# One whole load of the spatial bias, later MLP weights and regrouped token tiles in a planned two-layer kernel

## The chip, the cores and the metric

The kernel runs on one core of a Trainium2 chip. The metric is the device time of one execution in microseconds (us). The core has five engines with an instruction stream each: TensorE (PE, matrix products; its weight loads are listed apart as PEld), VectorE (DVE), ScalarE (ACT, activation functions), GpSimd (POOL) and SyncE (SP), which here issues all DMA transfers. Each engine works through its own stream strictly in the order in which it was written; streams meet through semaphores.

## The reference

Two layers follow each other, each an attention block and a gated MLP, both behind a layer norm and both added to x. The attention has 32 query heads of 16 columns that share one key and one value head. The MLP mixes tokens: one half of its GELU output is normalised and multiplied by a token-by-token matrix w_sp, to which a bias b_sp, one number for each token, is added. The same weights serve both layers.

```python
B, S, D, H = (1, 2048, 512, 32)          # Dh = 16, F = 1792, Fh = 896, all bf16
def _A_ref(x, wq, wk, wv, wo):
    q = (x @ wq).reshape(B, S, H, Dh)    # to b h s d
    k = x @ wk
    v = x @ wv
    scores = einsum('bhqd,bkd->bhqk', q, k) * Dh ** (-0.5)
    o = einsum('bhqk,bkd->bhqd', softmax(scores), v)
    return o.reshape(B, S, H * Dh) @ wo
def _B_ref(x, w_in, w_sp, b_sp, w_out):
    z = gelu(x @ w_in)
    z1 = z[..., :Fh]
    z2 = layernorm(z[..., Fh:])
    g = einsum('ts,bsf->btf', w_sp, z2) + b_sp[None, :, None]
    return (z1 * g) @ w_out
x = A_x
for _ in range(2):
    x = x + _A_ref(layernorm(x), A_wq, A_wk, A_wv, A_wo)
    x = x + _B_ref(layernorm(x), B_w_in, B_w_sp, B_b_sp, B_w_out)
```

## The kernel before

**An order written by a planner.** The Python code does not write instructions one after the other. It makes tasks with costs, dependencies and priorities, and a planner (`Sched`, `Kernel.run`) steps through a clock of its own, gives each free engine its next task, and so fixes the order of every engine's stream. On the chip only this order and the semaphores count. A table `PLAN` changes the planner's settings for single stretches of 1.25 us of its clock; it has some thousand rows. Some tasks have a gate: they may be placed only after a point of the planner's clock, such as `W_FROM` (the weights wo, w_in, w_out) and `WSP_FROM` (w_sp and the bias).

**Attention.** 2048 tokens are 16 tiles of 128. They are cut into chunks (`CHUNKS`), each chunk into units of 512 columns (tokens times head groups), 32 units a layer. A unit has 64 score blocks of 128 x 512, four for each tile of keys. PE computes up to four blocks side by side (L2468) into PSUM banks. About two thirds of the blocks go to ACT, which takes the exponential of two banks (L2666) or of one (L2665). The others go to DVE, which makes three integer ramps that together approximate the exponential: the first from PSUM (L2557, an "A" block), the other two by DVE or POOL from the first (L2577, L2561; two or four at once). All results land in a ring of P slots, `NPS` of 1 KB a partition (`Pb`). PE multiplies them by V, four at once in a "round" (L2725, PV). A finished unit is copied out of PSUM (oT, L1959), transposed by DMA (oP, L1634), divided by its denominators (L2105 on DVE, L2122 on POOL), transposed again (onT), multiplied by wo (L2065) and added to x. Then the second layer norm follows and a transpose into xnT. At the head of each layer the first layer norm's result xn is transposed by DMA into the space of z1 (`z<-xn`, L1634; the first two tiles on PE), and keys, values and queries are made from it (L1871, L1874, L1901).

**MLP stages.** When the chunks of a group (`GROUPS`) are through, an MLP stage runs for the group's tokens: PE multiplies by w_in (L2161 for z2, L2222 for z1) and ACT takes GELUs (L2166, L2236). Its table of functions is changed before and after (L2968). z1 is made for up to 512 tokens at a time, but never across a multiple of 512 tokens, since z1 and g lie in four token blocks tc. During a stage PE does not take up new scores. z2 is normalised (DVE L2174, POOL L2189) and kept in a ring of eight tiles (`Z2R`).

**Passes over w_sp.** The sum over the tokens s is cut into passes of two to four tiles (`PASSES`). A pass can start when its last group is through its stage. For each of the four token blocks tc and each of seven feature blocks f, PE multiplies the pass's z2 tiles by a slab of w_sp that DMA has brought in transposed (wstr, L1642), and DVE adds the result to g (L2290, `gp`). These products fill the gaps that attention leaves on PE. In the first pass the add takes the bias instead of the old g: `bspc` holds 512 tokens of it for all partitions, in one buffer, so that its four loads a layer (`L1627`) wait for one another:

```python
if pi == 0:
    lb = self.dma(self.bspc[:], self.B_b_sp[tc * 512:(tc + 1) * 512].partition_broadcast(P), 131072,
                  self.bs_use, prio=2, tag="ldb", gate=lambda: self.s.t > self.WSP_FROM)
```

The last pass of a layer (L2319, L2321, L2329, L2340) multiplies by z1, then w_out follows (L2350) and the add to x (L2354).

**SP's queue around the change.** In the program before, SP issues 13 of the 14 first transposes `z<-xn`, then wo, w_in, the last `z<-xn`, w_out, two oP, one onT, a slab of w_sp, the first quarter of the bias and another slab of w_sp. PE, DVE and SP keep this order whatever comes late.

Of the kernel before, what the change touches and what calls it, by code (L numbers as in the profile page):

```python
# [30 lines left out]
CHUNKS = (((0,128),(128,128),(256,256),(512,512),(1024,256),(1280,128),(1408,128),(1536,256),(1792,128),(1920,128)), ((0,128),(128,128),(256,256),(512,512),(1024,256),(1280,128),(1408,128),(1536,256),(1792,128),(1920,128)))  # L31
# [3 lines left out]
GROUPS = (((0,1,2),(3,),(4,5),(6,7),(8,9)), ((0,1,2),(3,),(4,5),(6,7),(8,9)))  # L35
PASSES = (((0,4),(4,8),(8,11),(11,14),(14,16)), ((0,4),(4,8),(8,11),(11,14),(14,16)))
# [34 lines left out]
def c_mm(n, cols):  # L71
# [15 lines left out]
    20: dict(SLACK_HI=800, FILL_MIN=4, PV_MAX=4, DVE_LEAD=300, POOL_TOP=2500, QUADP=0),
    21: dict(SLACK=350, PV_EFF=0.8),
    22: dict(SLACK=350, PV_LEAST=4, PV_EFF=0.8),
    23: dict(SLACK=350, ACT_LOW=700, PV_LEAST=4, PV_EFF=0.8, COLS=0),  # L90
    24: dict(SLACK=350, ACT_LOW=1400, PV_LEAST=4, PV_EFF=0.8, COLS=0),
    25: dict(SLACK=200, DVE_LEAD=-300, POOL_TOP=2500, SCORE_CAP=5),
    26: dict(SLACK=200, DVE_LEAD=-300, POOL_TOP=3500, SCORE_CAP=5),
    27: dict(SLACK=200, DVE_LEAD=-300, POOL_TOP=3500, SCORE_CAP=5),
    28: dict(SLACK=200, DVE_LEAD=-300, POOL_TOP=3500, MISC_T=700, ACT_MAX=1, SCORE_CAP=5),
    29: dict(SLACK=200, DVE_LEAD=-300, MISC_T=700, ACT_MAX=1, SCORE_CAP=5),
    30: dict(SHARE=0.31, POOL_TOP=2500),
    31: dict(SHARE=0.45, POOL_TOP=2500, QUADP=0),
    32: dict(FILL_MIN=4, PV_EFF=0.8),
    33: dict(PV_LEAST=4, QUADP=0),  # L100
    34: dict(PV_LEAST=4, QUADP=0),
    35: dict(PV_LEAST=4, SHARE=0.4, MISC_T=2500, QUADP=0),
    36: dict(ACT_LOW=1700, PV_LEAST=4, PV_EFF=0.8, SHARE=0.4, MISC_T=2500, DVE_HIGH=2400, QUADP=0),
    37: dict(ACT_LOW=1700, PV_LEAST=4, PV_EFF=0.8, SHARE=0.4, POOL_TOP=2500, MISC_T=2500, DVE_HIGH=2400, QUADP=0),
    38: dict(ACT_LOW=1700, PV_LEAST=4, PV_EFF=0.8, SHARE=0.4, POOL_TOP=2500, MISC_T=2500, SCORE_CAP=5, DVE_HIGH=2400, QUADP=0),
    39: dict(ACT_LOW=1700, PV_LEAST=4, PV_EFF=0.8, SHARE=0.45, POOL_TOP=2500, MISC_T=2500, SCORE_CAP=5, DVE_HIGH=2400, QUADP=0, QUADD=0),
    40: dict(PV_LEAST=8, SHARE=0.31, SCORE_CAP=7, DVE_HIGH=1200),
    42: dict(PV_LEAST=4),
    43: dict(SLACK_HI=300, PV_EFF=0.8, MISC_T=700, DVE_HIGH=1200),
    44: dict(SLACK_HI=300, PV_EFF=0.8, MISC_T=700, DVE_HIGH=1200),  # L110
    45: dict(SLACK_HI=300, PV_EFF=0.8, MISC_T=700, DVE_HIGH=1200),
    46: dict(SLACK_HI=300, PV_EFF=0.8, POOL_TOP=2500, MISC_T=2500, DVE_HIGH=2400),
    47: dict(POOL_TOP=2500),
    48: dict(POOL_TOP=2500),
    49: dict(FILL_BUSY=3, DVE_LEAD=-300, HOLD=400),
    51: dict(FILL_BUSY=3, SHARE=0.28, POOL_TOP=3500, HOLD=400),
    52: dict(FILL_BUSY=3, SHARE=0.28, POOL_TOP=3500, HOLD=400, ACT_MAX=1),
    53: dict(POOL_TOP=7000),
    54: dict(POOL_TOP=7000),
    55: dict(SLACK=450, SLACK_HI=400, PV_LEAST=8, POOL_TOP=3500, SCORE_CAP=7),  # L120
    56: dict(SLACK=450, SLACK_HI=400, PV_LEAST=8, POOL_TOP=3500, SCORE_CAP=7),
    57: dict(SLACK=450, SLACK_HI=400, PV_LEAST=8, POOL_TOP=3500, SCORE_CAP=7),
    58: dict(SLACK=450, SLACK_HI=400, ACT_LOW=1400, PV_LEAST=8, POOL_TOP=3500, SCORE_CAP=7, QUADD=0),
    59: dict(SLACK=450, SLACK_HI=650, ACT_LOW=1400, PV_MAX=1, PV_LEAST=8, POOL_TOP=3500, SCORE_CAP=7, QUADD=0),
    60: dict(SLACK=450, SLACK_HI=650, ACT_LOW=1400, FILL_BUSY=3, PV_MAX=1, PV_LEAST=8, POOL_TOP=3500, SCORE_CAP=7, DVE_HIGH=1200, QUADD=0),
    61: dict(SLACK=450, SLACK_HI=650, ACT_LOW=1400, FILL_BUSY=3, PV_MAX=1, PV_LEAST=8, POOL_TOP=3500, SCORE_CAP=7, DVE_HIGH=1200, QUADD=0),
    63: dict(ACT_MAX=1),
    64: dict(ACT_LOW=900, PV_MAX=4, SHARE=0.28, HOLD=0, MISC_T=700),
    65: dict(MISC_T=2500, COLS=0),
    66: dict(COLS=0),  # L130
    67: dict(COLS=0),
    68: dict(PV_MAX=3),
    69: dict(ACT_LOW=700, PV_MAX=3, DVE_HIGH=1200),
    70: dict(ACT_LOW=700, PV_MAX=3, MISC_T=2500, ACT_MAX=1, DVE_HIGH=1200),
    72: dict(SLACK=200, ACT_LOW=500, PV_MAX=1, DVE_LEAD=300, POOL_TOP=7000),
    73: dict(SLACK=200, ACT_LOW=1700, PV_MAX=4, DVE_LEAD=300, POOL_TOP=3500),
    74: dict(ACT_LOW=1700, PV_MAX=3, DVE_LEAD=300, POOL_TOP=3500),
    75: dict(ACT_LOW=1050, PV_MAX=1, POOL_TOP=2500, HOLD=400, QUADD=0),
    76: dict(ACT_LOW=1400, PV_MAX=1, POOL_TOP=2500, HOLD=400, QUADD=0),
# [24 lines left out]
    106: dict(ACT_LOW=1050, SHARE=0.4, POOL_TOP=2500, HOLD=400, DVE_HIGH=2400),
    107: dict(SLACK_HI=300, PV_MAX=4, PV_EFF=0.8),
    108: dict(SLACK_HI=300, PV_MAX=4, PV_EFF=0.8, POOL_TOP=2500),
    109: dict(SLACK_HI=300, PV_MAX=4, PV_EFF=0.8, POOL_TOP=2500, SCORE_CAP=5),
    110: dict(SLACK=600, SLACK_HI=650, FILL_MIN=3, SHARE=0.45),
    111: dict(SLACK=450, SLACK_HI=650, FILL_MIN=3, SHARE=0.45, QUADP=0),
    112: dict(SLACK=350, SLACK_HI=650, FILL_MIN=3, SHARE=0.45, COLS=3300, QUADP=0),  # L170
    113: dict(SLACK=350, SLACK_HI=650, FILL_MIN=3, SHARE=0.45, POOL_TOP=7000, COLS=3300, QUADP=0),
    114: dict(SLACK=350, SLACK_HI=650, FILL_MIN=3, PV_LEAST=4, SHARE=0.45, POOL_TOP=7000, COLS=3300, QUADP=0),
    115: dict(SLACK=350, SLACK_HI=650, FILL_MIN=3, PV_LEAST=4, SHARE=0.45, POOL_TOP=7000, COLS=3300, QUADP=0),
    116: dict(SLACK=350, SLACK_HI=650, ACT_LOW=1400, FILL_MIN=3, PV_LEAST=4, SHARE=0.45, POOL_TOP=7000, COLS=3300, DVE_HIGH=1200, QUADP=0),
    117: dict(SLACK_HI=800, FILL_MIN=3, POOL_TOP=3500, SCORE_CAP=7),
    118: dict(SLACK_HI=800, FILL_MIN=3, DVE_LEAD=300, POOL_TOP=3500, SCORE_CAP=7),
    119: dict(SLACK_HI=800, FILL_MIN=3, DVE_LEAD=300, POOL_TOP=3500, ACT_MAX=1, SCORE_CAP=7),
    121: dict(SLACK_HI=800, POOL_TOP=3500),
    122: dict(SLACK_HI=800, PV_EFF=0.8, POOL_TOP=3500, MISC_T=2500),
# [1283 lines left out]
class Kernel:  # L1463
# [794 lines left out]
    def spatial(self, B, pi, final):  # L2258
# [5 lines left out]
        for tc in range(4):  # L2264
# [6 lines left out]
            else:  # L2271
# [4 lines left out]
                for f in range(NF):  # L2276
# [17 lines left out]
                    if pi == 0:  # L2294
                        self.bs_use.append(outs[0])
# [873 lines left out]
```

## Time and profile before

| what | value |
|---|---|
| median of three runs (lowest, highest) | 1503.27 us (1502.33, 1505.92) |
| the profiled execution | 1499.42 us, span 1497.7 us |
| score blocks to ACT: L2666, two at a time | 1212 instructions, 1154.3 us busy |
| score blocks to ACT: L2665, one at a time | 339 instructions, 205.8 us busy |
| score blocks to DVE: L2557 | 1333 instructions, 858.2 us busy |
| z1 on PE, L2222 of 512, 384, 256, 128 columns | 112, 56, 112, 56 matmuls; 25.6, 9.9, 12.9, 3.5 us busy |
| bias loads | 8 of 128 KB, 3.7 us each from issue to landing |
| w_in and w_out loads | 1792 KB in 9.1 us, 896 KB in 7.2 us |
| first matmul of the first MLP stage | at 213.5 us |

A group of the profile names the line, the engine, the output and input tiles, the shapes and the count, then the busy time and the idle time before it. "Idle before" is time in which the engine stood still in front of that instruction, and the releaser behind the arrow is what ended the wait. Matmuls overlap, so busy time divided by count is shorter than the mean duration of one. The granted clock is the share of full speed that the clock of PE had in a window. The two long chains in the time are the attention of layer 0, to about 695 us, and of layer 1, to about 1436 us; behind each lies the rest of the MLP.

### The profile page before, as it was taken

The numbers are of one execution on the slowest core, as the hardware profiler recorded it, in microseconds if no ns is written. First come the engines' busy times: TensorE is split into PE (matmuls) and PEld (weight loads), VectorE is DVE, ScalarE is ACT, GpSimd is POOL, SyncE is SP. The second block draws the span as 40 slices with busy tenths as digits, with TensorE's granted clock in tenths as the row PEclk, the third lists the DMA queues.
The fourth block names the chain that finished last, engine by engine and source line by source line (L and its number), as shares of the span: only waits on it lengthen the run. The fifth ranks groups of instructions, "written<-read, shape, count | busy, mean of one in ns | idle before, by whom it ended". The sixth has DMA issues, their size and how long they took to land.

```text
span 1497.7 us, 35502 instructions
## 1 busy us (share of the span) xinstructions
PE 1433.2 (96%) x14120; PEld 473.1 (32%) x14120; DVE 1383.0 (92%) x2605; ACT 1377.4 (92%) x1725; POOL 1037.3 (69%) x1152
## 2 busy tenths in 40 slices
PE   8999899999999999999999988999999999999999
PEld 3332232222322322233643322322223223222345
DVE  8899998999899999989767999899998999999886
ACT  7999999999999999996589999999999999999950
POOL 6677768878688688864114767677776786888737
PEclk9999999999999999999999999999999999999999
DMA  4420001112011111112121001001111111211111
GB/s 111 114 43 12 9 18 26 26 26 40 18 26 33 23 32 30 37 20 40 21 41 32 16 12 16 15 23 26 26 37 19 30 33 19 44 30 28 28 33 57
DMA packets 156627, 47.55 MB, mean 32 GB/s; under 512 B 148913, under 2 KB 155953, under 8 KB 156465
## 3 DMA queue, kind: packets, MB, share of 16 engines
q1 hardware_dynamic: 156464, 45.28, 15.2%
q8 instruction: 115, 1.88, 0.5%
q14 instruction: 48, 0.39, 0.1%
HBM read 6.98 MB, written 2.10 MB: 6 GB/s over the span
## 4 chain that ended last, share of the span: by engine, by line
ACT 53%; PE 36%; DVE 7%; DMA 2%; issue 0%; POOL 0%; SPq 0%; DVEq 0%
ACT Pb L2666 46%; PE ps_all L2725 9%; PE ps_all L2468 9%; PE ps_all L2280 7%; ACT Pb L2665 6%; DVE Pb L2557 4%; PE ps_all L2161 3%; PE ps_all L2350 3%; PE ps_all L2222 3%; PE ps_all L2321 1%; DMA bspc<-in_B_b_sp_dram 1%; DVE Pb L2577 1%; DMA z<-xn 1%; DVE gp L2290 1%; ACT L2968 1%
## 5 line engine op out<-in xcount | busy, mean ns | idle before, releaser
L2666 ACT ACTIVATE Pb<-ps_all 128x1024 bf16<-128x1024 f32 x1212 | 1154.3, 1138 | 12.8 <-PE ps_all L2468 11.9
L2577 POOL TENSOR_SCALAR Pb<-Pb 128x1024 int16<-128x1024 int16 (+1 forms) x732 | 803.4, 1097 | 212.0 <-DVE Pb L2577 163.4
L2557 DVE TENSOR_SCALAR Pb<-ps_all 128x512 int16<-128x512 f32 x1333 | 858.2, 684 | 39.7 <-PE ps_all L2468 33.6
L2468 PE MATMUL ps_all<-z,kT 32*128 32x512 bf16 x4096 | 535.8, 385 | 45.3 <-ACT Pb L2666 25.4
L2725 PE MATMUL ps_all<-Pb,V 128*32 128x512 bf16 x6762 | 531.9, 385 | 4.2 <-DVE Pb L2557 1.0
L2468 PEld LDWEIGHTS ps_all<-z,kT 32*128 32x128 bf16 x4096 | 136.2, 91 | 570.6 <-ACT Pb L2666 393.5
L2280 PE MATMUL ps_all<-wstr,z 128*128 128x512 bf16 x784 | 224.1, 384 | 1.8 <-DVE gp L2290 1.4
L2665 ACT ACTIVATE Pb<-ps_all 128x512 bf16<-128x512 f32 x339 | 205.8, 719 | 6.1 <-PE ps_all L2468 5.9
L2577 DVE TENSOR_SCALAR Pb<-Pb 128x1024 int16<-128x1024 int16 (+1 forms) x451 | 195.7, 471 | 0.4
L2725 PEld LDWEIGHTS ps_all<-Pb,V 128*32 128x32 bf16 x6762 | 124.6, 94 | 225.9 <-issue 119.5
L2290 DVE TENSOR_TENSOR gp<-ps_all,gp 128x512 f16<-128x512 f32 x168 | 113.2, 683 | 1.2 <-PE ps_all L2280 0.8
L2280 PEld LDWEIGHTS ps_all<-wstr,z 128*128 128x128 bf16 x784 | 51.5, 97 | 93.8 <-issue 41.7
L1724 POOL TENSOR_SCALAR ln_rs<-ln_mv 128x1 f32<-128x1 f32 (+2 forms) x52 | 11.6, 225 | 97.2 <-DVE ln_mv L1734 90.4
L2561 POOL TENSOR_SCALAR Pb<-Pb 128x512 int16<-128x512 int16 x79 | 48.8, 617 | 40.3 <-DVE Pb L2577 22.3
L2350 PE MATMUL ps_all<-w_out,z 128*128 128x512 bf16 x224 | 58.4, 380 | 0.3 <-DVE z L2329 0.2
L2122 POOL TENSOR_TENSOR o_norm<-oP,rdn 128x128 bf16<-128x128 bf16 (+1 forms) x84 | 39.7, 495 | 21.4 <-DVE Pb L2577 12.1
L2161 PE MATMUL ps_all<-w_in,xnT 128*128 128x448 bf16 x256 | 53.2, 353 | 0.9 <-ACT xnT L1785 0.7
L2222 PE MATMUL ps_all<-xnT,w_in 128*128 128x512 bf16 (+3 forms) x336 | 51.5, 308 | 0.0
L2174 DVE BATCH_NORM_STATS2 st<-z 128x6 f32<-128x448 bf16 x64 | 35.6, 604 | 13.8 <-ACT z L2166 13.6
L1959 DVE CAST oT<-ps_all 128x512 bf16<-128x512 f32 x64 | 43.9, 686 | 4.2 <-PE ps_all L2725 4.1
L1733 DVE BATCH_NORM_STATS2 ln_st<-X 128x6 f32<-128x512 bf16 x64 | 43.3, 682 | 1.7 <-DMA X<-in_A_x_dram 1.5
L2236 ACT ACTIVATE z<-ps_all 128x512 bf16<-128x512 f32 (+2 forms) x62 | 31.4, 562 | 13.7 <-PE ps_all L2222 13.6
(76 smaller groups left out, 768.4 us busy)
## 6 DMA issues: line engine op xcount, KB each, us to landing
out_dram<-X SPq DMA_DIRECT2D x16, 128.0 KB, 1.7
w_in<-in_B_w_in_dram SPq DMA_DIRECT2D x1, 1792.0 KB, 9.1
X<-in_A_x_dram SPq DMA_DIRECT2D x3, 512.0 KB, 7.8
bspc<-in_B_b_sp_dram SPq DMA_DIRECT2D x8, 128.0 KB, 3.7
oP<-oT SPq DMA_TRANSPOSE x60, 2.4
w_out<-in_B_w_out_dram SPq DMA_DIRECT2D x1, 896.0 KB, 7.2
wstr<-in_B_w_sp_dram SPq DMA_TRANSPOSE x40, 4.1
X<-in_A_x_dram SPq DMA_DIRECT2D x2, 256.0 KB, 3.2
```

The costliest lines, as they stand in the source:

```text
L2161: ins = e.matmul(self.ps32[:, b, 0:448], self.xnT2[:, buf, kd, o:o + P], self.w_in[:, kd, FH + h * 448:FH + (h + 1) * 448], start=(kd == 0 ...
L2222: ins = e.matmul(self.ps32[:, b, i * nq:(i + 1) * nq], self.w_in[:, kd, f * P:(f + 1) * P], self.xnT2[:, buf, kd, x0:x0 + nq], start=(kd = ...
L2280: ins = e.matmul(self.ps32[:, b, :], self.z2[:, (s0 + i) % Z2R, f * P:(f + 1) * P], self.wstr[:, sl[i // SLAB][1] + i % SLAB, :], start=(i ...
L2290: return Task("dve", c_ps(512), lambda e: e.tensor_tensor(self.gp[:, tc, f, :], self.ps32[:, bank(), :], src, ALU.add), dps, self.GP_P, ta ...
L2350: ins = e.matmul(self.ps32[:, b, :], self.z1[:, tc, f, o:o + P], self.w_out[:, f, :], start=(f == 0), stop=(f == NF - 1))
L2468: ins = e.matmul(self.ps32[:, jb[i].i, :], self.kT[32 * j:32 * j + 32, u.half, kt * P:(kt + 1) * P], q, tile_position=(32 * j, 0), start=T ...
L2557: return lambda e: e.tensor_scalar(self.Pi[:, dst(), :], self.ps32[:, bank, :], EBIAS + lo, lo, op0=ALU.add, op1=ALU.max)
L2561: return lambda e: e.tensor_scalar(self.Pi[:, dst(), :], self.Pi[:, src(), :], lo, 1.0, op0=ALU.add, op1=ALU.mult)
L2577: return lambda e: e.tensor_scalar(self.several(self.Pi, dst), self.several(self.Pi, src), lo, 1.0, op0=ALU.add, op1=ALU.mult)
L2665: return e.activation(self.Pb[:, ss[0], :], self.ps32[:, bs[0], :], ACTF.Exp, scale=ESCALE)
L2666: return e.activation(self.two(self.Pb, *ss), self.two(self.ps32, *bs), ACTF.Exp, scale=ESCALE)
L2725: ins = e.matmul(self.ps32[32 * j:32 * j + 32, u.bank.i, :], self.V[:, var, kt, :], self.Pb[:, sl.i, :], tile_position=(0, 32 * j), start= ...
```

## The change

The bias is loaded once for the whole kernel, all 2048 tokens (512 KB), into a buffer four times as large; the first pass reads its quarter from it. The P ring shrinks from 44 to 41 slots. wo may be placed from 48,000 ns of the planner's clock instead of 45,000, and w_in and w_out, like the bias, from 75,000. The planner's cost of a w_sp transfer on SP is another formula. Chunks, groups and passes are cut anew, in both layers: the groups were 4, 4, 3, 3 and 2 tiles (the bounds in tokens 512, 1024, 1408, 1792, 2048) and are 3, 4, 4, 3 and 2 (384, 896, 1408, 1792, 2048); the passes are the same tiles. No chunk of 512 tokens is left. `PLAN` has other rows. Since the planner places everything again, the whole order differs.

```diff
-CHUNKS = (((0,128),(128,128),(256,256),(512,512),(1024,256),(1280,128),(1408,128),(1536,256),(1792,128),(1920,128)), ...
+CHUNKS = (((0,128),(128,256),(384,128),(512,256),(768,128),(896,128),(1024,256),(1280,128),(1408,128),(1536,256),(1792,128),(1920,128)), ...
-GROUPS = (((0,1,2),(3,),(4,5),(6,7),(8,9)), ((0,1,2),(3,),(4,5),(6,7),(8,9)))
-PASSES = (((0,4),(4,8),(8,11),(11,14),(14,16)), ((0,4),(4,8),(8,11),(11,14),(14,16)))
+GROUPS = (((0,1),(2,3,4),(5,6,7),(8,9),(10,11)), ((0,1),(2,3,4),(5,6,7),(8,9),(10,11)))
+PASSES = (((0,3),(3,7),(7,11),(11,14),(14,16)), ((0,3),(3,7),(7,11),(11,14),(14,16)))
 PLAN = {
...
 }
...
-    W_FROM = 45000
-    NPS = 44
+    W_FROM = 48000
+    NPS = 41
...
-        self.bspc = self.sb([P, 512], BF16, "bspc")
+        self.bspc = self.sb([P, S], BF16, "bspc")
...
     def dma_w(self, dst, src, nbytes, deps=(), prio=5, tag="dmat", gate=None):
         def cost():
-            occ = 1000 + nbytes / 610.0
+            occ = 1230 + 600 * max(0.0, nbytes / 131072 - 2.7)
...
         self.ldo = self.dma(self.wo[:], self.A_wo.rearrange("(c p) n -> p c n", p=P), 524288, prio=2.5, gate=late)
-        self.ldin = self.dma(self.w_in[:], self.B_w_in.rearrange("(kd p) f -> p kd f", p=P), 1835008, prio=2.5, gate=late)
-        self.ldout = self.dma(self.w_out[:], self.B_w_out.rearrange("(c p) n -> p c n", p=P), 917504, prio=2.5, gate=late)
+        def later():
+            return s.t > self.WSP_FROM
+        self.ldin = self.dma(self.w_in[:], self.B_w_in.rearrange("(kd p) f -> p kd f", p=P), 1835008, prio=2.5, tag="ldb", gate=later)
+        self.ldout = self.dma(self.w_out[:], self.B_w_out.rearrange("(c p) n -> p c n", p=P), 917504, prio=2.6, tag="ldb", gate=later)
+        self.ldbs = self.dma(self.bspc[:], self.B_b_sp.partition_broadcast(P), 524288, prio=2.4, tag="ldb", gate=later)
...
                 if pi == 0:
-                    lb = self.dma(self.bspc[:], self.B_b_sp[tc * 512:(tc + 1) * 512].partition_broadcast(P), 131072,
-                                  self.bs_use, prio=2, tag="ldb", gate=lambda: self.s.t > self.WSP_FROM)
-                    self.bs_use = []
+                    lb = self.ldbs
...
-                        src = self.bspc[:] if pi == 0 else self.gp[:, tc, f, :]
+                        src = self.bspc[:, tc * 512:(tc + 1) * 512] if pi == 0 else self.gp[:, tc, f, :]
...
-                    if pi == 0:
-                        self.bs_use.append(outs[0])
```

More of the change, by code (lines that the diff above doesn't have):

```diff
@@ L87 @@
[L87 to L103, printed above, removed]
@@ L1127 @@
-    1190: dict(SLACK=150, ACT_LOW=900, PV_LEAST=4),
+    1: dict(FILL_MIN=4),
+    2: dict(FILL_MIN=4),
+    3: dict(FILL_MIN=4),
+    4: dict(FILL_MIN=4),
+    5: dict(FILL_MIN=4),
+    6: dict(FILL_MIN=4),
+    7: dict(FILL_MIN=4),
+    8: dict(FILL_MIN=4),
+    9: dict(ACT_LOW=900),
+    10: dict(ACT_LOW=900),
+    11: dict(ACT_LOW=900, COLS=3300, QUADP=0),
+    12: dict(ACT_LOW=700, FILL_BUSY=3, COLS=3300, QUADP=0),
+    13: dict(ACT_LOW=1700, PV_EFF=0.8),
+    15: dict(SLACK=600),
+    16: dict(SLACK=600, POOL_TOP=2500, HOLD=400, SCORE_CAP=5),
@@ new lines @@
+    158: dict(ACT_MAX=1),
+    159: dict(FILL_BUSY=3),
+    160: dict(SLACK_HI=800, PV_LEAST=4),
+    161: dict(SLACK_HI=800, ACT_LOW=1050, PV_LEAST=4, ACT_MAX=1, SCORE_CAP=5),
+    162: dict(ACT_LOW=700, PV_MAX=4, POOL_TOP=2500, HOLD=0),
+    164: dict(SHARE=0.24, MISC_T=700),
+    165: dict(SHARE=0.24, MISC_T=700),
+    166: dict(FILL_BUSY=4, HOLD=400),
+    167: dict(MISC_T=700),
+    168: dict(MISC_T=700),
+    169: dict(PV_MAX=1, PV_EFF=0.8),
+    171: dict(ACT_LOW=500),
+    172: dict(ACT_LOW=900, DVE_LEAD=300),
@@ new lines @@
+    191: dict(SCORE_CAP=5),
+    192: dict(SCORE_CAP=5),
+    193: dict(PV_MAX=1, MISC_T=2500, SCORE_CAP=5),
+    194: dict(SLACK=350, FILL_MIN=4, SCORE_CAP=5, COLS=3300),
+    195: dict(SLACK=350, FILL_MIN=4, PV_LEAST=4, DVE_LEAD=-300, COLS=3300, DVE_HIGH=2400),
+    196: dict(POOL_TOP=3500),
+    197: dict(ACT_LOW=900, PV_LEAST=8, POOL_TOP=7000),
+    198: dict(PV_LEAST=4),
+    200: dict(SLACK_HI=400, HOLD=0, MISC_T=700, SCORE_CAP=7),
+    202: dict(ACT_LOW=700),
+    204: dict(FILL_BUSY=3, COLS=2900),
@@ new lines @@
+    331: dict(PV_MAX=1),
+    334: dict(ACT_LOW=1400, FILL_MIN=4, HOLD=400, SCORE_CAP=7),
+    335: dict(COLS=0, DVE_HIGH=2400),
+    336: dict(ACT_LOW=700, FILL_BUSY=3, POOL_TOP=3500),
+    338: dict(DVE_HIGH=2400),
+    340: dict(ACT_LOW=1050, SHARE=0.28, MISC_T=2500),
+    341: dict(QUADD=0),
+    342: dict(COLS=2900),
+    343: dict(SLACK_HI=650, POOL_TOP=2500, COLS=2900),
+    344: dict(FILL_BUSY=3, PV_LEAST=8),
+    345: dict(SLACK=200, FILL_BUSY=3, PV_LEAST=8, MISC_T=700),
+    346: dict(SLACK=200, FILL_BUSY=3, PV_LEAST=8, MISC_T=700),
@@ new lines @@
+    363: dict(SLACK_HI=300),
+    364: dict(SLACK_HI=300, FILL_MIN=3, PV_MAX=3, HOLD=400, MISC_T=700),
+    367: dict(FILL_MIN=4, DVE_LEAD=-600, QUADP=0),
+    368: dict(SLACK_HI=400),
+    369: dict(SLACK=450, PV_LEAST=4),
+    370: dict(SHARE=0.36, POOL_TOP=2500, MISC_T=700, QUADP=0),
+    371: dict(PV_MAX=1),
+    372: dict(PV_MAX=1, POOL_TOP=2500),
+    373: dict(PV_MAX=4),
+    374: dict(SLACK_HI=400, PV_MAX=4, HOLD=0, MISC_T=2500),
+    375: dict(PV_LEAST=4, PV_EFF=0.8, QUADD=0),
+    376: dict(PV_LEAST=8, SHARE=0.31, DVE_LEAD=-600, MISC_T=700),
@@ new lines @@
+    508: dict(ACT_LOW=700),
+    509: dict(FILL_MIN=3),
+    510: dict(FILL_MIN=3),
+    511: dict(FILL_MIN=3),
+    512: dict(FILL_MIN=3, DVE_LEAD=-300, QUADP=0),
+    513: dict(ACT_LOW=1700, FILL_MIN=3, DVE_LEAD=-300, QUADP=0),
+    514: dict(DVE_LEAD=-600),
+    515: dict(POOL_TOP=7000),
+    516: dict(FILL_BUSY=3, POOL_TOP=7000, QUADP=0),
+    517: dict(SLACK_HI=400, FILL_BUSY=3, POOL_TOP=7000, QUADP=0),
+    519: dict(FILL_BUSY=3, PV_MAX=3, DVE_LEAD=-300, QUADP=0),
+    520: dict(COLS=2900),
@@ new lines @@
+    536: dict(FILL_MIN=4),
+    537: dict(FILL_MIN=4),
+    538: dict(PV_LEAST=4, POOL_TOP=7000),
+    539: dict(PV_LEAST=4, POOL_TOP=7000, HOLD=400, SCORE_CAP=7),
+    540: dict(PV_LEAST=4, SHARE=0.45, POOL_TOP=7000, HOLD=400),
+    541: dict(SLACK=150, PV_LEAST=4, SHARE=0.45, POOL_TOP=7000),
+    542: dict(PV_LEAST=8, SHARE=0.4),
+    543: dict(ACT_LOW=500, QUADD=0),
+    544: dict(FILL_MIN=4),
+    545: dict(FILL_MIN=4, ACT_MAX=1, QUADP=0),
+    546: dict(DVE_HIGH=2400),
+    547: dict(SLACK=600),
@@ new lines @@
+    577: dict(SLACK_HI=800, PV_LEAST=4, DVE_LEAD=-300, POOL_TOP=7000, HOLD=400),
+    579: dict(SLACK=150),
+    580: dict(SLACK=150),
+    581: dict(ACT_MAX=1),
+    582: dict(PV_MAX=1, POOL_TOP=7000, DVE_HIGH=2400),
+    584: dict(DVE_LEAD=-300),
+    585: dict(DVE_LEAD=-300),
+    586: dict(PV_LEAST=8),
+    587: dict(SLACK=350, PV_MAX=1, SHARE=0.4, DVE_LEAD=-300, HOLD=0, MISC_T=2500, ACT_MAX=1),
+    588: dict(SLACK=350, FILL_MIN=3, PV_MAX=1, SHARE=0.4, HOLD=0),
+    589: dict(FILL_MIN=3, PV_MAX=1, SHARE=0.4, HOLD=0),
@@ new lines @@
+    762: dict(QUADP=0),
+    763: dict(HOLD=400, QUADP=0),
+    764: dict(HOLD=400, SCORE_CAP=7, COLS=3300, QUADP=0),
+    765: dict(ACT_LOW=500, PV_LEAST=8, DVE_LEAD=300),
+    766: dict(PV_MAX=3, DVE_HIGH=2400),
+    767: dict(HOLD=0, QUADD=0),
+    768: dict(PV_LEAST=8, HOLD=0, SCORE_CAP=5, DVE_HIGH=1200),
+    769: dict(PV_LEAST=8, HOLD=0, ACT_MAX=1, SCORE_CAP=5, DVE_HIGH=1200),
+    770: dict(PV_MAX=1),
+    771: dict(PV_MAX=1, PV_LEAST=4, SHARE=0.36),
+    772: dict(FILL_MIN=3, PV_MAX=1),
@@ L1128 @@
+    1187: dict(SLACK_HI=300, DVE_LEAD=-600),
+    1188: dict(SLACK_HI=300, DVE_LEAD=-600),
+    1189: dict(SLACK_HI=300, DVE_LEAD=-600),
+    1190: dict(SLACK_HI=300, DVE_LEAD=-600),
+    1191: dict(SLACK_HI=300, DVE_LEAD=-600, POOL_TOP=2500),
+    1192: dict(DVE_LEAD=300, ACT_MAX=1),
+    1193: dict(DVE_LEAD=300, ACT_MAX=1),
 }
```

2010 lines of the change are left out of this document (975 added, 1035 removed).

## The prediction, made before the result was known

> **What bounds the kernel now.** I read the busy times first, then what ScalarE (ACT) waits for, then ten-microsecond windows where it is not full.
>
> ```profile
> PE 1433.2 (96%) x14120; PEld 473.1 (32%) x14120; DVE 1383.0 (92%) x2605; ACT 1377.4 (92%) x1725; POOL 1037.3 (69%) x1152
> ...
> ACT  7999999999999999996589999999999999999950
> ```
>
> PE, DVE and ACT are all above 90%, and ACT is below nine tenths only in the first slice, at the change of layer (slices 19 to 21) and at the end. Between these the exponentials follow each other without a gap, so this stretch ends when ACT has done its share; PE has room there (47.88 of 50 us busy from 100 to 150, 44.41 from 150 to 200, with ACT at 50.00 in both). The windows in which ACT nevertheless falls short, outside the GELU stages:
>
> ```profile
> 50.00:60.00 10.00, 7.77 (x80) 1.93 (x77) 6.28 (x14) 7.09 (x9) 4.31 (x6) 0.83 0.53 105
> 260.00:270.00 10.00, 8.81 (x94) 2.20 (x86) 9.01 (x17) 8.95 (x11) 5.81 (x6) 1.00 0.04 14
> 320.00:330.00 10.00, 8.89 (x94) 2.18 (x86) 9.14 (x16) 9.50 (x12) 7.46 (x8) 1.00 0.01 3
> 1000.00:1010.00 10.00, 8.51 (x73) 1.90 (x69) 7.87 (x14) 7.71 (x9) 5.79 (x6) 0.83 0.02 4
> 1060.00:1070.00 10.00, 8.52 (x87) 2.08 (x87) 8.62 (x17) 8.75 (x11) 6.74 (x7) 1.00 0.03 8
> sum 50.00, PE 42.50 PEld 10.29 DVE 40.92 ACT 42.01 POOL 30.11; mean PE 8.50 PEld 2.06 DVE 8.18 ACT 8.40 POOL 6.02
> ```
>
> The columns are the length, then busy time of PE, PEld, DVE, ACT and POOL, the granted clock, the DMA share and GB/s. ACT loses 50.00 - 42.01 = 8.0 us in the five. The order of events shows why, in the first and in the fourth:
>
> ```profile
> 42.75 0.50 SPq L1627 DMA_DIRECT2D w_in<-in_B_w_in_dram  x1
> 46.61 1.20 SPq L1634 DMA_TRANSPOSE z<-xn  x1
> 52.52 0.38 PE L1871 MATMUL ps_all<-z,wk 128*128 128x128 bf16 x4 [1.93 <-DMA z<-xn]
> 53.35 0.60 ACT L2665 ACTIVATE Pb<-ps_all 128x512 bf16<-128x512 f32 x1 [1.79 <-PE ps_all L2468]
> ...
> 996.56 0.59 SPq L1627 DMA_DIRECT2D bspc<-in_B_b_sp_dram  x1
> 1001.06 0.69 DVE L2290 TENSOR_TENSOR gp<-ps_all,bspc 128x512 f16<-128x512 f32 x1 [1.78 <-DMA bspc<-in_B_b_sp_dram]
> 1001.81 0.60 PE L2280 MATMUL ps_all<-wstr,z 128*128 128x512 bf16 x2 [1.41 <-DVE gp L2290]
> 1002.93 1.94 ACT L2666 ACTIVATE Pb<-ps_all 128x1024 bf16<-128x1024 f32 x2 [1.33 <-PE ps_all L2468]
> ```
>
> The last transpose of the first normalisation goes out behind the 1.8 MB of w_in and lands about 5.8 us later (median of its kind 2.5); PE, which runs in order, waits for that tile's keys, and ACT for PE. At 996 the next quarter of the bias can be fetched only once its one buffer is read out. DVE, in order too, waits, its A blocks (L2557) queue behind it, PE gets no bank, ACT no scores. After both waits the granted clock is 0.83 in the window.
>
> **The change part by part.**
>
> *Bias whole.* Eight loads of 128 KB become one of 512 KB that waits for nothing; the chain of work that ended last passes through five of the old ones. What ACT lost behind four of these is in the windows: 1.05 + 0.50 + 2.29 + 1.25 = 5.1 us. I take all of it: ACT has no spare time around them with which to make it good. At least 0 comes back (if other work is late at the same spot), at most what DVE lost in the four, 0.99 + 0.86 + 2.13 + 1.38 = 5.4.
>
> *Weights later.* In the changed program all 14 first transposes stand ahead of wo on SP's queue, and w_in and w_out come only after wo, two oP transposes, one onT, the first two slabs of w_sp and the bias. The first wait and the slow clock behind it go: 10.00 - 7.09 = 2.9 us; bounds 0 and DVE's 3.7. Queued behind the three loads are the next oP transpose (86.09 now) and an xnT transpose. The loads take 9.1 (w_in) and 7.2 (w_out) to land, the bias between 3.7 and four times that, 14.8: 20 to 31 us, begun at about 75, so this oP lands at 95 to 106. DVE's reciprocal needs it together with its pair's second transpose, which goes out at 104.21 now and lands 2.4 later: hidden. Without that cover, a late oP would hold DVE and cost what the bias waits cost, 1 to 3 us. The first MLP stage, at 213.5 now, comes one token tile earlier, and a tile takes ACT some 40 us (an estimate: 1212 x 2 + 339 blocks in 32 tiles, 86 a tile, at 0.459), so w_in is there 60 us ahead.
>
> *Groups of 3, 4, 4, 3, 2 tiles instead of 4, 4, 3, 3, 2.* The same multiset, so ten GELU stages, twenty table loads and the last two stages of each layer stay. But a four-tile group now straddles a 512-token border, so z1 takes 112 matmuls of 384 and 112 of 128 columns in place of 112 of 512. By their groups, 9.9/56 and 3.5/56 against 25.6/112: 19.8 + 7.0 - 25.6 = +1.2 us. This lies on the path, because ACT waits for PE in these stages (13.6 us on L2222 in all). The 28 GELUs of 512 become 28 of 384 and eight small ones, +0.8 us on ACT (23.4/42 and 7.1/16 us each), hidden in those same waits; 0.8 if not.
>
> *Passes.* The first pass now starts after three tiles and the four-tile third pass is released late. The order of the changed program shows what is left over: behind the last score of layer 0 stand 57 matmuls of the spatial sum instead of 54, behind that of layer 1, 60 instead of 57. At 0.216 us each (24 in 5.18 us on the chain at 702) that is 0.65 a layer, 1.3 us, which I count, as the chain runs over L2280 there; 0 if the wait for the last group's inputs hides them.
>
> *Three P slots fewer* (44 to 41). The program now has 1186 paired and 387 single exponentials instead of 1212 and 339. Back to back, 41 pairs took 37.63 and 5 singles 2.46 us on the chain: -26 x 0.918 + 48 x 0.492 = -0.3 us; by group means (0.952, 0.607) +4.4. I take -0.3, since they do run back to back.
>
> *The rest.* Score packs 1393 to 1399 and PV rounds 1768 to 1760, so PE's share is even (-2 x 0.216 us). DVE gets 4 more A blocks (0.644 each), 8 more paired and 3 more quadruple ramps (0.404, 0.694): +7.9 us on an engine idle for 115 us; nothing, but up to 4 if half of it met ACT's pace. POOL gives up ramps and is 69% busy: nothing.
>
> **Sum.** -5.1 - 2.9 + 1.2 + 1.3 - 0.3 = -5.8 us. The profiled execution took 1499.42 us (span 1497.7): 1493.6. The runs shown have their median 3.85 us above that, so 1503.27 - 5.8 = 1497.5.
>
> [...]
>
> **Rivals.**
>
> *New waits for the old ones.* Every instruction's place is new, and a transfer whose use is planned some 4 us behind its issue can come late anywhere: most reciprocals stand that close to their oP transposes. Against it: now no DVE row waits on oP at all. If half the gain is lost, 1497.5 + 4.0 = 1501.5.
>
> *The slow clock stays* for reasons of its own. The idle ACT time behind the two waits, 0.48 + 0.64 and 0.40 + 0.48 = 2.0 us, stays: 1499.5. [...] The row against it is the clock of 1.00 in every fifty-microsecond window between 100 and 1000.
>
> *The late tile (slower).* After token 1408 nine tiles of the spatial sum are still to do, not eight, and PE is busy 49.78 of 50 us from 550 to 600. If none of that tile fits beside the attention, each layer's end grows by 28 x 0.216 = 6.0 us: 1497.5 + 12.1 = 1509.6. The kernel is no faster from the point where 5.8 us, 27 of the 56 matmuls, are left over beyond the six I counted, and slower by 0.3% from 10.3 us, 48 of them. Against it: only three more stand there in the program.
>
> *The slots (slower too).* With three slots fewer ACT can run ahead of PE by 3 x 0.459 us less at each of ten stages: at most 13.8 us, 1511.3. Against: no row of ACT waits for a PV matmul now, and the planner placed its work with 41.
>
> That the change does not do what it says is ruled out by the program: no instruction of the first pass waits for a load behind a gp add any more.
>
> **How the numbers follow.** Forecast 0.64 (its own range 1493 to 1500), new waits 0.18, slow clock 0.05, late tile 0.07, slots 0.06. A measurement of this kernel tells about 0.3% from no change, 4.5 us: faster means below 1498.8, slower above 1507.8. Faster: nine tenths of the forecast, a fifth of the new waits, two fifths of the slow clock: 0.63. Slower: most of the last two, 0.11. The same: 0.26. The range goes from 1492 (DVE's 5.4 + 3.7 = 9.1 us won, the costs hidden, and 1.8 for half the spread of the runs shown: 1503.3 - 9.1 - 0.3 - 1.8) to 1505 (new waits that take all of the 8.0: 1505.5); the two slow cases lie outside.
>
> **What would show it.** Right: no row in which DVE waits for bspc; ACT above 9.9 in the window from 50 to 60; clock 1.00 in all windows between 20 and 690; ACT's busy time within 5 us of now; PE waits on L2222 a little longer in the four-tile stages. Wrong: DVE or PE rows that wait for oP, onT, xnT or wstr; ACT waiting for L2725; more than 60 L2280 matmuls between ACT's last exponential of a layer and the last group's L2161; a second half-rate stretch.

## The result and the profile after

The changed kernel takes 1488.42 us (median of four runs, 1487.81 to 1488.78), beside 1503.32 us for the kernel before in the same comparison: a ratio of 0.9898, with a 95% interval from 0.9881 to 0.9915, 14.9 us less. The profiled execution took 1488.28 us (span 1486.5). So the direction was right and the size wrong: 1497.5 was predicted, and the time lies below the range.

The page of the changed kernel, in the parts that were shown of the kernel before (busy time by engine, and ACT in 40 slices):

```profile
PE 1431.1 (96%) x14232; PEld 480.4 (32%) x14232; DVE 1386.6 (93%) x2620; ACT 1376.5 (93%) x1755; POOL 1032.8 (69%) x1161
...
ACT  7999999999999999996689999999999999999950
```

No engine does noticeably less: ACT's busy time falls by 0.9 us, while the span falls by 11.2. What went is idle time of ACT. The same five windows in the changed kernel (columns as in the prediction):

```profile
50.00:60.00 10.00, 9.90 (x121) 3.94 (x121) 8.86 (x19) 8.90 (x15) 6.53 (x9) 1.00 0.06 18
260.00:270.00 10.00, 9.78 (x95) 2.64 (x92) 10.00 (x17) 10.00 (x12) 9.29 (x10) 1.00 0.22 50
320.00:330.00 10.00, 7.91 (x91) 2.09 (x88) 9.93 (x19) 10.00 (x13) 7.77 (x10) 1.00 0.21 28
1000.00:1010.00 10.00, 9.05 (x99) 2.62 (x95) 10.00 (x21) 10.00 (x14) 6.77 (x9) 1.00 0.77 120
1060.00:1070.00 10.00, 8.59 (x107) 2.50 (x103) 10.00 (x20) 10.00 (x15) 7.49 (x10) 1.00 0.14 27
```

ACT, in the fourth busy column, is full in the four windows of the bias, and the granted clock is 1.00 in all five. In the first window ACT lacks 1.10 us, so one sign of the prediction (ACT above 9.9 there) did not come. The order of events there shows a wait that the new order itself makes:

```profile
55.50 1.15 ACT L2706 ACTIVATE Pb<-ps_all 128x1024 bf16<-128x1024 f32 x1
...
56.32 1.05 PE L2765 MATMUL ps_all<-Pb,V 128*32 128x512 bf16 x16
56.52 0.68 DVE L1956 TENSOR_SCALAR z<-ps_all 128x512 bf16<-128x512 f32 x1
...
57.30 0.10 PEld L2508 LDWEIGHTS ps_all<-z,kT 32*128 32x128 bf16 x4 [0.42 <-DVE z L1956]
57.30 0.39 PE L2508 MATMUL ps_all<-z,kT 32*128 32x512 bf16 x4
...
57.75 1.02 ACT L2706 ACTIVATE Pb<-ps_all 128x1024 bf16<-128x1024 f32 x1 [1.10 <-PE ps_all L2508]
```

PE has just made a tile of queries (L1945), which DVE copies until 57.20 (L1956); meanwhile PE works off four rounds of P times V (L2765). The next scores (L2508) start only behind both, and their weight load was released by that copy, so ACT stands for 1.10 us. No transfer is late there. How long ACT waited for scores in all, before and then after (total, times, longest):

```profile
ACT Pb L2666 <- PE ps_all L2468: 11.9, 17, 1.4
ACT Pb L2665 <- PE ps_all L2468: 5.9, 8, 1.8
```

```profile
ACT Pb L2706 <- PE ps_all L2508: 5.8, 9, 1.4
ACT Pb L2705 <- PE ps_all L2508: 2.8, 5, 0.9
```

17.8 us became 8.6, a difference of 9.2; 8.0 of it had been foreseen.

### The profile page after: what moved, and what is told of

Same layout as the page of the kernel before. It is cut to its first block, busy times and chain, and to the rows that moved or that the text cites. A ratio compares the mean times of both kernels' runs of the same rounds, so it can differ in the third digit from the quotient of the medians.

```text
span 1486.5 us, 35825 instructions
## 1 busy us (share of the span) xinstructions
PE 1431.1 (96%) x14232; PEld 480.4 (32%) x14232; DVE 1386.6 (93%) x2620; ACT 1376.5 (93%) x1755; POOL 1032.8 (69%) x1161
## 4 chain that ended last, share of the span: by engine, by line
ACT 72%; PE 21%; DVE 5%; DMA 1%; issue 0%; POOL 0%; POOLq 0%
ACT Pb L2706 62%; ACT Pb L2705 8%; PE ps_all L2205 3%; DVE Pb L2597 3%; PE ps_all L2508 3%; PE ps_all L2765 3%; PE ps_all L2322 3%; PE ps_all L2266 3%; PE ps_all L2390 3%; PE ps_all L2361 1%; DVE Pb L2617 1%; PE ps_all L1945 1%; DMA z<-xn 1%; ACT L3008 1%; PE ps_all L2359 0%; DVE gp L2332 0%
## 5 line engine op out<-in xcount | busy, mean ns | idle before, releaser
L2706 ACT ACTIVATE Pb<-ps_all 128x1024 bf16<-128x1024 f32 x1186 | 1135.3, 1153 | 6.3 <-PE ps_all L2508 5.8
L2508 PE MATMUL ps_all<-z,kT 32*128 32x512 bf16 x4096 | 536.4, 384 | 40.8 <-ACT Pb L2706 23.0
L2765 PE MATMUL ps_all<-Pb,V 128*32 128x512 bf16 x6770 | 530.6, 384 | 2.8 <-ACT Pb L2706 0.8
L2508 PEld LDWEIGHTS ps_all<-z,kT 32*128 32x128 bf16 x4096 | 136.4, 90 | 564.1 <-ACT Pb L2706 375.8
L2705 ACT ACTIVATE Pb<-ps_all 128x512 bf16<-128x512 f32 x387 | 235.8, 719 | 3.0 <-PE ps_all L2508 2.8
L2617 DVE TENSOR_SCALAR Pb<-Pb 128x1024 int16<-128x1024 int16 (+1 forms) x462 | 198.8, 466 | 0.3
L2765 PEld LDWEIGHTS ps_all<-Pb,V 128*32 128x32 bf16 x6770 | 125.7, 94 | 225.3 <-issue 118.2
L1763 POOL TENSOR_SCALAR ln_rs<-ln_mv 128x1 f32<-128x1 f32 (+1 forms) x56 | 12.4, 224 | 93.6 <-DVE ln_mv L1773 87.7
L2601 POOL TENSOR_SCALAR Pb<-Pb 128x512 int16<-128x512 int16 x69 | 42.8, 620 | 37.2 <-DVE Pb L2597 14.7
L2266 PE MATMUL ps_all<-xnT,w_in 128*128 128x128 bf16 (+2 forms) x448 | 52.3, 273 | 0.0
L2280 ACT ACTIVATE z<-ps_all 128x384 bf16<-128x384 f32 (+2 forms) x70 | 32.7, 517 | 13.4 <-PE ps_all L2266 13.4
```

Source lines behind the costliest of these rows:

```text
L2266: ins = e.matmul(self.ps32[:, b, i * nq:(i + 1) * nq], self.w_in[:, kd, f * P:(f + 1) * P], self.xnT2[:, buf, kd, x0:x0 + nq], start=(kd = ...
L2508: ins = e.matmul(self.ps32[:, jb[i].i, :], self.kT[32 * j:32 * j + 32, u.half, kt * P:(kt + 1) * P], q, tile_position=(32 * j, 0), start=T ...
L2617: return lambda e: e.tensor_scalar(self.several(self.Pi, dst), self.several(self.Pi, src), lo, 1.0, op0=ALU.add, op1=ALU.mult)
L2705: return e.activation(self.Pb[:, ss[0], :], self.ps32[:, bs[0], :], ACTF.Exp, scale=ESCALE)
L2706: return e.activation(self.two(self.Pb, *ss), self.two(self.ps32, *bs), ACTF.Exp, scale=ESCALE)
L2765: ins = e.matmul(self.ps32[32 * j:32 * j + 32, u.bank.i, :], self.V[:, var, kt, :], self.Pb[:, sl.i, :], tile_position=(0, 32 * j), start= ...
```

## The experiments

The kernels of the table ran on three chips. Since the granted clock of each run turned out to matter, the table gives it. "At clock 1.000" is the end of a straight line through the runs of a kernel, time against granted clock; the runs scatter around the line by 0.4 to 1.1 us (standard deviation), and its end is good to 0.2 to 0.8 us. For the changed kernel nearly all runs were there anyway.

| chip | kernel | runs | mean clock | median, us | at clock 1.000, us |
|---|---|---|---|---|---|
| first | before | 24 | 0.9950 | 1500.99 | 1497.3 |
| first | bias ahead | 11 | 0.9971 | 1493.52 | 1491.7 |
| first | w_in later | 12 | 0.9981 | 1495.43 | 1493.9 |
| first | both | 6 | 0.9973 | 1490.97 | 1489.4 |
| first | changed kernel, w_in early | 8 | 0.9959 | 1495.59 | 1492.1 |
| second | before | 11 | 0.9944 | 1502.64 | 1496.5 |
| second | changed kernel again | 6 | 0.9997 | 1487.76 | 1487.8 |
| third | before | 21 | 0.9947 | 1501.05 | 1496.5 |
| third | before, kept warm | 12 | 0.9982 | 1497.79 | 1496.4 |
| third | both, kept warm | 8 | 0.9989 | 1489.81 | 1489.6 |
| third | both, again | 8 | 0.9984 | 1489.23 | 1489.2 |

### The loads alone, in the old order

The first three kernels keep the order of every engine of the kernel before and mend only the loads. For the bias:

```diff
-        self.bspc = self.sb([P, 512], BF16, "bspc")
+        self.bspc = self.sb([P, 1024], BF16, "bspc")
...
+                    m = 4 * B.layer + tc
+                    if m == 0:
+                        bdst, bsrc = self.bspc[:], self.B_b_sp[0:1024]
+                    else:
+                        q = (m + 1) % 4
+                        bdst, bsrc = self.bspc[:, q % 2 * 512:q % 2 * 512 + 512], self.B_b_sp[q * 512:(q + 1) * 512]
...
```

Each add waits for the load one before. The second buffer takes 1 KB more for each partition; small statistics tiles that now share space give back a part of it.

> The kernel before with the order of every engine's instructions kept; only the bias comes one quarter earlier, into two buffers of 1 KB, so that no first-pass add waits for the load issued just before it. Theory A (the waits for the bias cost what they show in the profile, and in addition make the clock fall at a place and for a length that differs from run to run): profile at least 5 us shorter, about 1494; no DVE row that waits for bspc; clock 1.00 around 1000; and the timed runs shorter by more than that, 6 to 9 us, because part of the 3.9 us between the profile and the median of the kernel before goes away. Theory B (the waits cost just the 5.1 us seen in the one profile, the 3.9 us are something else): profile about 1494.3 and median about 1498.2. Theory C (another thing is late at the same place): profile at 1497 or above, ACT still short in the windows around these four places.

The ratio to the kernel before is 0.9952 (0.9935 to 0.9969), 5.6 us less at clock 1.000, where 5.1 was expected. The median is 7.5 us lower and the profiled execution took 1493.43 us: as theory A has it, not theory B or C. No DVE row waits for bspc any more, and the window from 1000 to 1010 has ACT at 10.00 and the clock at 1.00. The other wait is still there, and its window shows more than before:

```profile
50.00:60.00 10.00, 7.71 (x66) 1.77 (x66) 5.17 (x12) 6.07 (x7) 3.71 (x5) 0.68 0.33 93
```

In this execution ACT lost 3.93 us there instead of 2.91, with a clock of 0.68 instead of 0.83. The half-rate stretch behind this wait is 6.83 us long here; it was 3.41 us in the kernel before.

For w_in, one entry moves on SP's queue:

```diff
+        p = self.s.prog["sp"]
+        i = next(i for i, x in enumerate(p) if x[3] is self.ldin)
+        w, fn, key, tk = p.pop(i)
...
+        p.insert(i + 1, (w, fn, key, tk))
```

> The kernel before with one move on SP's queue: the last transpose of the first normalisation ahead of w_in instead of behind it, all else in the old order. Theory A: the wait of PE at 52.5 and the half-rate stretch behind it go, 2.9 us in the profile (1496.5), and 3 to 5 us in the median of the timed runs. Theory B: 2.9 us in both. Theory C (a new wait takes its place, as the changed kernel has one at 57.75): ACT still short by 1 us or more in the window from 50 to 60, gain 1.8 us or less. The clock is 1.00 from 50 to 60 by A and B.

Ratio 0.9965 (0.9949 to 0.9980), 3.4 us at clock 1.000, and 5.6 us by the medians, somewhat more than theory A had; ACT has 10.00 in the window from 50 to 60 and the clock 1.00, so no new wait takes this one's place.

> Both edits above together on the kernel before: no new groups, no new plan. Theory A: profile about 8 us shorter than the kernel before (1491.4), timed runs 9 to 12 us shorter, so median and profile within 1 us of each other as they are in the changed kernel, and about 3 us left to the new plan. Theory B: profile 1491.4 and median 1495.3, 8 us shorter; then 7 us of the changed kernel's 14.9 are the new plan's and the new groups'. Theory D (the gain is the plan's, the waits are made good elsewhere): less than 4 us.

Ratio 0.9934 (0.9909 to 0.9959); on the third chip 0.9931 (0.9905 to 0.9957). By the medians the two edits bring 10.0 and 11.8 us, within theory A's 9 to 12; at clock 1.000 they bring 7.9 and 7.3 us. Theory D falls. So the loads alone also win back much of the clock: its mean is 0.9973 and 0.9984, beside 0.9950 and 0.9947 for the kernel before. But the first chip's profiled execution took 1494.07 us, above the kernel's median, and has two half-rate stretches in new places, one from 16 to 23 us and one behind 1125. Windows of it around the second, with the same columns:

```profile
1122.00:1124.00 2.00, 1.14 (x8) 0.38 (x8) 2.00 (x5) 2.00 (x4) 1.83 (x3) 1.00 0.33 66
1124.00:1126.00 2.00, 2.00 (x19) 0.54 (x22) 1.98 (x4) 2.00 (x5) 1.92 (x2) 0.82 1.02 70
1126.00:1128.00 2.00, 2.00 (x17) 0.27 (x13) 1.17 (x3) 1.75 (x4) 1.84 (x2) 0.50 0.40 74
1128.00:1130.00 2.00, 2.00 (x12) 0.23 (x4) 1.62 (x5) 1.58 (x4) 0.54 (x2) 0.50 0.00 0
1130.00:1132.00 2.00, 2.00 (x8) 0.69 (x8) 1.33 (x4) 1.67 (x3) 0.75 (x1) 0.50 0.00 0
```

PE was busy for only 1.14 of 2 us, with two short waits, 0.26 and 0.53 us; then the clock is 0.50, and ACT runs short (1.17 of 2 us). The kernel with w_in later shows a stretch at the same place, the kernel before and, on the third chip, the kernel with both loads passed it at full clock in their profiled executions. No transfer ended a wait there, so neither load has to do with it.

### The changed kernel with w_in early

```diff
+        p = self.s.prog["sp"]
+        j = [i for i, x in enumerate(p) if x[3].tag == "TA"][13]
+        i = next(i for i, x in enumerate(p) if x[3] is self.ldin)
+        w, fn, key, tk = p.pop(i)
...
+        p.insert(j, (w, fn, key, tk))
```

> The changed kernel with w_in put back on SP's queue ahead of the last transpose of the first normalisation, all else as changed. If that order is what made the wait: PE waits for the transpose by about 1.9 us again, half-rate clock in the window from 50 to 60, 2 to 3 us slower than the changed kernel in the profile (1490 to 1491), 3 to 5 in the timed runs (1491.5 to 1493.5). If the last transpose has slack in the new plan (its keys stand later in the order): no wait, within 0.7 us of the changed kernel.

1495.59 us, 7.8 above the changed kernel's median on the second chip, more than either theory gave. The wait is longer than in the kernel before, and a half-rate stretch of 10.24 us goes with it; the row is PE's:

```profile
53.63 0.58 PE L1915 MATMUL ps_all<-z,wk 128*128 128x128 bf16 x4 [4.08 <-DMA z<-xn]
```

Every one of its eight runs has a clock of 0.998 or less. At clock 1.000 the order costs 4.3 us; that is across two chips, and 0.8 us uncertain, since no run came near that clock. The collision makes a wait of 4.08 us in the new order, where it was 1.93 in the old one, and of the 7.8 us the slower clock takes 3.5, about as much as the wait.

### The changed kernel once more, and without the planner's rows

> The changed kernel once more, beside the kernel before on one chip, for the granted clock of every run. Theory A (the changed kernel has lost the dips of PE that make the clock fall): mean clock 0.999 or 1.000 in nearly all runs, span 1486 to 1488, median and profile within 1 us, while the runs of the kernel before spread over clocks from 0.988 to 0.999 as in the last call. Theory E (the four runs of the changed kernel were on a chip that throttles less): its runs spread over several us too, with clocks down to 0.995, and the difference to the kernel before shrinks to about 9 us, what is left of it at clock 1.0.

Ratio 0.9903 (0.9881 to 0.9926). Five of its six runs have a clock of 1.000 and one 0.998; the kernel before, beside it, lies between 0.990 and 0.999. Theory A holds, theory E falls.

The next three have no rows; the last, made from the changed kernel, has the old CHUNKS, GROUPS and PASSES besides.

```diff
-PLAN = {
...
-}
+PLAN = {}
...
-GROUPS = (((0,1),(2,3,4),(5,6,7),(8,9),(10,11)), ((0,1),(2,3,4),(5,6,7),(8,9),(10,11)))
-PASSES = (((0,3),(3,7),(7,11),(11,14),(14,16)), ((0,3),(3,7),(7,11),(11,14),(14,16)))
+GROUPS = (((0,1,2),(3,),(4,5),(6,7),(8,9)), ((0,1,2),(3,),(4,5),(6,7),(8,9)))
+PASSES = (((0,4),(4,8),(8,11),(11,14),(14,16)), ((0,4),(4,8),(8,11),(11,14),(14,16)))
```

> The kernel before with the planner's tuned rows taken away (PLAN empty): all its waits and loads stay, the order is the planner's own. If the tuned rows are worth much: 1510 to 1530. It is the base for the next two.

> The changed kernel with the tuned rows taken away: whole bias, later weights, new groups and passes, 41 slots, the planner's own order. Theory P (what the changed kernel has beyond the waits, and its steadier clock, come from its new tuned rows): against the kernel before without rows it gains at clock 1.0 only the waits, 6 to 9 us, or less. Theory G (the new groups have a worth of their own): more than 9 us.

> As the last, but with the groups, passes and chunks of the kernel before: whole bias, later weights and 41 slots alone, no tuned rows. Theory P: 6 to 9 us faster at clock 1.0 than the kernel before without rows, and within 2 us of the changed kernel without rows. Theory G: at least 3 us slower than the changed kernel without rows. If the prediction's costs of the groups (1.2 + 1.3 us) are real: about 2.5 us faster than it.

Medians 1562.01, 1569.27 and 1552.36 us; spans at clock 1.000: 1554.2, 1562.0 and 1548.7. The first is far above the 1510 to 1530 expected. Without rows the loads with 41 slots win 5.5 us, a little less than expected. The new groups lose 13.3, where theory P had at most 2 and the prediction's costs 2.5; one wait is a large part of it (PE's row in the changed kernel without rows):

```profile
743.60 1.67 PE L1114 MATMUL ps_all<-w_in,xnT 128*128 128x448 bf16 x4 [6.48 <-DMA xnT<-xn]
```

So the groups have no worth of their own that shows without rows: theory G falls. Neither do these runs price them in the tuned kernel, since the rows are worth some 60 us on one order and 76 on the other, far more than the effect in question.

### What makes the clock fall

> A kernel that computes nothing of the model: it leaves out everything but the loads of x and wo, and its output is x. PE runs trains of about 12 us, first of the attention's kind (four 32-row matmuls, then four of 32 columns), then of full 128x128 matmuls with 512 columns; after each train it waits for one DVE fill of 64, 300, 600, 900, 1200, 1600, 2000 or 2600 columns, eight times each, and then come groups of 3 and 4 fills of 200 columns with two short units of PE work between them. [...] If the kind of matmul counts (quarter arrays less than full ones), the first half falls earlier than the second.

A gap is one DVE fill that waits for the train's last matmul and that the next train waits for:

```diff
+        for unit, per in ((mix, 0.43), (full, 0.43)):
+            for n in (64, 300, 600, 900, 1200, 1600, 2000, 2600):
+                for i in range(8):
+                    w = gap(n)
+                    train(unit, int(12.0 / per), w)
```

A train of the attention's kind took 17.8 us, not 12, since its unit takes 0.65 us. One gap on PE, and two windows that each hold a gap of this length and the train behind it; the engines in the windows are PE, PEld, DVE and POOL:

```profile
645.00 0.39 PE L2047 MATMUL ps_all<-X,wo 32*128 32x512 bf16 x4 [1.45 <-DVE Pb L2067]
```

```profile
643.90:664.50 20.60, 19.14 (x216) 5.54 (x216) 1.07 (x2) 0.00 (x0) 0.92 0.00 1
...
685.10:704.30 19.20, 17.80 (x216) 5.49 (x216) 1.05 (x1) 0.00 (x0) 1.00 0.01 2
```

The same gap of 1.45 us is followed by a half-rate stretch once (0.92 over the gap and the train) and by none another time (1.00). So many of the eight gaps of each length were followed by one, in the one execution profiled, with a mean clock of 0.977:

| PE idle, us | 0.3, 0.5, 0.8 | 1.1 | 1.4 | 1.9 | 2.3 | 2.9 |
|---|---|---|---|---|---|---|
| attention's kind (quarter-array matmuls) | 0 | 0 | 2 | 6 | 6 | 8 |
| full 128x128 matmuls | 0 | 0 | 0 | 0 | 2 | 5 |

Each stretch lasted 3.41 us, or 6.83, as in the kernels. Three or four gaps of about 0.4 us with some work between were never followed by one. The kind of matmul counts, too: behind gaps of 1.9 us the clock fell in six cases of eight in the attention's kind of work and in none in full matmuls, behind 2.3 us in six and in two. What in a wait decides whether the clock falls is not shown: of eight gaps of 1.45 us two were followed by a stretch and six were not. Nor is the changed kernel proof against the fall: two of its ten runs have clocks of 0.999 and 0.998.

To test whether work in the waits keeps the clock up, PE was given some there, of the sort that the planner itself uses (L2856: matmuls with zeros that add nothing to a bank of P times V):

```diff
+            def fn(e, u=u, js=js, r=r):
+                for _ in range(r):
+                    for j in js:
+                        e.matmul(self.ps32[32 * j:32 * j + 32, u.bank.i, :], self.zero[:], self.wq[:, 0, :],
+                                 tile_position=(0, 32 * j), start=False, stop=False)
+            p.insert(i, ([], fn, None, None))
```

> The kernel before with all its loads and waits where they were, and its own kind of idle work for PE added: four 128x32 matmuls with zeros that add nothing to a bank of P times V, 8 rounds ahead of the keys' matmul that waits behind w_in, 5 rounds ahead of each of the two PE instructions that wait behind the bias at about 1001 and 1062, and, at 1119 to 1124, 3 rounds and three full matmuls into banks that scores overwrite next. Theory T (the clock falls because the array does too little in these waits): the waits stay, ACT still loses some 5 to 8 us of busy time to them, but the clock in the timed runs goes from 0.995 on average to 0.998 or more, and the median falls by 2 to 4 us, to 1497 to 1499. [...]

> The kernel with both loads mended (bias ahead, w_in later), and with the idle work of the last one at 1119 to 1124 alone. Theory T: no half-rate stretch at about 1125 any more, clocks of 0.998 to 1.000, median 1488.5 to 1490 instead of 1491, so that what is left to the new groups and rows is about 1 us. [...]

> The kernel with both loads mended once more, beside the two others on one chip: median about 1491, clocks from 0.991 to 1.000, the half-rate stretch at 1125 in the profile again or not, by chance.

The kernel before, kept warm, takes 1497.79 us, a ratio of 0.9969 (0.9950 to 0.9989): 3.3 us are won by matmuls that compute nothing. Its waits are still there: DVE waits three times for the bias, 3.0 us instead of 5.6 in four, and ACT lacks 1.99 us from 50 to 60, now at full clock:

```profile
50.00:60.00 10.00, 8.99 (x116) 2.79 (x108) 7.42 (x15) 8.01 (x12) 5.19 (x9) 1.00 0.32 94
```

At clock 1.000 it equals the kernel before (1496.4 and 1496.5), so the clock makes the whole difference. The numbers came as theory T had them: the mean clock is 0.9982, where the kernel before has 0.9947 on the same chip. The kernel with both loads, kept warm, shows no gain over the same kernel without that work (1489.81 and 1489.23); there the test says nothing, since on this chip that kernel kept its clock in six of eight runs by itself.

## Why the prediction failed

**The largest step that failed is the last of the sum:** "The runs shown have their median 3.85 us above that, so 1503.27 - 5.8 = 1497.5." I took the distance between the profiled execution and the median as a constant of the measurement. It was part of what the change removes. The forecast missed by 9.1 us: 3.7 of them are this step (3.85 less the 0.14 that the changed kernel has), the other 5.3 lie between the two profiled executions, in the terms further down. The kernel before runs at a mean clock of 0.995, and each thousandth costs it 0.9 to 1.1 us; its profiled execution, at 0.998, was one of its better ones. The changed kernel stays at 1.000 in eight of its ten runs (0.998 and 0.999 in the others), so there median and profile agree to 0.14 us. By the table the clock is worth 4 to 6 us to the kernel before (median less the time at clock 1.000); the prediction had counted 2.0 of it, as the price of "The slow clock stays". It is shown that the clock costs this and that work in the waits gives part of it back, 3.3 us. The code held a hint that I had passed over: the planner itself places matmuls with zeros (L2856) where PE would do too little by its settings. What the planner cannot see, such as a wait for a late load, it does not fill.

**Bias and weights, -5.1 and -2.9: right, a little small.** The loads alone gave 5.6 and 3.4 us at full clock, and 7.3 to 7.9 together; the two terms, without the 2.0 us of slow clock that they hold, come to 6.0. In the changed kernel the new 1.10 us wait at 57.75 takes some of the second back, and the transfers behind the three loads are hidden, as counted: no DVE row waits for oP, onT or bspc.

**z1 in two pieces, +1.2 on the path: wrong.** The z1 matmuls did grow, from 51.5 to 52.3 us by their groups, 0.8. But the four stages of four tiles, from the first table load to the first exponential behind it, took 49.35 us in all before and 49.04 after; ACT's wait for L2266 is 13.4 us, where it was 13.6 for L2222.

**Matmuls left over, +1.3: wrong size.** The end of layer 0 took 37.48 us before and 37.47 after, that of layer 1 62.17 and 62.45: +0.27. The matmuls behind the last score did become 57 and 60, but most of the addition leaves no trace in these times; what covers it was not followed up.

**Exponentials, -0.3: too small.** ACT's busy time in the attention outside the GELU stages fell by 0.9 us in layer 0 and 1.2 in layer 1. A further 2.0 us came from the start of layer 1 (ACT idle 7.09 us there before, 5.13 after), which no term of mine held. With these, the attention outside the stages is 4.7 us shorter in layer 0 and 6.9 in layer 1; the stages and ends add 0.6, and the start of the kernel takes 0.1 off: together the span's 11.2. Of the 5.3 us that the sum missed, 1.9 are thus costs that did not come (2.5 counted, 0.6 seen), 1.8 the exponentials and 2.0 the start of layer 1; the rest is small and goes both ways.

**The gain in parts, at the medians:** some 4 to 6 us from the clock, 7.3 from the two loads at full clock (1496.5 to 1489.2), and 1.4 from groups, slots and rows together (1489.2 to 1487.8, on two chips whose kernels before agree at 1496.5 at clock 1.000). In the comparison of the result the two last would leave 6.2 of the 14.9 for the clock. How the 1.4 splits is not settled, nor whether one of these edits or all keep PE busy from 1120 to 1130, where it has 10.00 of 10 us in the changed kernel and 9.02 in the kernel before.

**The rivals.** Of the new waits, one of more than 1 us came, at 57.75. The slow clock did not stay; the sentence on it was turned the wrong way, as a risk to 2.0 us and not as a stake of 4 to 6. The late tile and the slots did not show: ACT waits less for scores than before, 8.6 us.

No experiment pointed to a kernel that would beat the changed one by more than could be measured; outside the first slice of 37 us, the GELU stages and the start of layer 1, the 1.10 us at 57.75 is ACT's longest wait left.

## What to carry to other kernels

A wait can cost more than its length when a half-rate stretch follows it, as with the wait of 4.08 us here, which had 10.24 us at half rate behind it and came with 7.8 us in the median. Compare the granted clocks of several runs, not of one profile, and work out how time depends on the clock before you carry an offset over. A distance between profile and median is a finding to explain. In a planned order, a wait that the planner doesn't know is also a wait that it doesn't fill; take it away or put harmless matmuls into it, which won 3.3 us here.

## What was not expected of the hardware

The clock of PE halved for 3.41 us behind two of eight gaps of 1.45 us in quarter-array work; in full-array work it did so behind none of eight of 1.9 us and two of eight of 2.3 us. No run shows why. What one program gets differs from run to run, too: the kernel before had clocks from 0.988 to 0.999 in 24 runs on one chip, and times from 1497.0 to 1508.8 us.
